# A fused attention and feed-forward kernel: first pair's K side split, loads reordered and released by a new gate, small fillers, joined bursts for all f32-loaded pairs

## The chip, the cores and the metric

One core of one Trainium2 chip runs the whole program. The metric is the device time of one execution in microseconds; "span" is the time from the first to the last instruction of the profiled execution, about 2 us shorter. The kernel before takes 322.0 us (median of 3 runs, 320.87 to 322.46).

## The reference

Random-feature attention (Performer) over 8 batches x 8 heads, then a feed-forward layer with a quick GELU. Two heads make a "pair"; there are 32 pairs, four to a batch.

```python
def phi(x):                       # per pair: K and Q sides
    h = x @ omega.T - sum(x*x)/2;  h = h - max(h)
    return exp(h) / sqrt(m)
kv  = einsum('bhsm,bhsd->bhmd', k_p, v);  z = sum(k_p)
out = einsum('bhsm,bhmd->bhsd', q_p, kv) / (einsum('bhsm,bhm->bhs', q_p, z) + 1e-6)
# then, on x of 4608 x 512:
h = x @ w_in                      # 512 -> 2048
y = (h * sigmoid(1.702 * h)) @ w_out
```

## The kernel before

A scheduler inside the kernel plans, on the host, the order in which each engine gets its instructions; the program is then recorded in that order, and each engine runs its own list strictly in order. A planned order is therefore fixed: an instruction whose data is late holds up everything behind it on its engine. The names of the operations are those of the plan: TK and TQ (transposes of pair i), K and Q (its feature matmuls), KV, ND (numerator and denominator), m1 and m2 (the two feed-forward matmuls, 292 groups of mostly four), hk, hq, hv (f32 loads of a pair), TD (transpose of a pair by DMA), ld (a load on GpSimd's software queue, cast on the way for q, k and weights).

K, Q and KV use half of the array's rows ("tiled"); changing between them and the rest costs time, so they are put in bursts. `mates` says who must stand together:

```python
JOIN, AHEAD = 16, 2
LOADS = [("k", 1), ("q", 1), ("k", 2), ("q", 2), ("k", 3), ("q", 3), ("v", 0), ("v", 1), ("v", 2), ("v", 3)]
LOADS += [("wi", j) for j in range(4)]
LOADS += [(x, i) for i in range(4, 8) for x in "kqv"] + [("wo", j) for j in range(4)]
BEGIN, SPACING = 8, 8        # K of pair i not before so many feed-forward groups
# ...
    def mates(o):
        kind, i = o[0], o[1]
        if kind in ("Q", "KV") and i >= EARLY:
            k = [("K", i + AHEAD)] if JOIN <= i < NPAIR - AHEAD else []
            return k + ([("KV", i)] if kind == "Q" else [("Q", i)] if k else [])
        if kind == "K" and JOIN + AHEAD <= i:
            return [("Q", i - AHEAD), ("KV", i - AHEAD)]
        return []
```

So from pair 16 on, Q and KV of pair i stand in one burst with K of pair i+2. Pairs 1 to 7, v of pair 0 and all weights come through the software queue; k and q of pair 0 and pairs 8 to 31 come as f32 through SP's hardware queue (q of pair 0 through ScalarE's) and are cast by ScalarE or VectorE. The f32 loads begin behind a gate:

```python
deps["gate", 8] = [("ld", "wo", 0)]
# ...
def gate():
    stg[EARLY] = stgp.tile([128, 2 * S], F32, name="stg", tag="stg")
    nc.sync.dma_start(stg[EARLY][:].bitcast(BF16)[:, 2 * S : 2 * S + 2], wout[:, 0, 0:2])
```

The tiny transfer reads the first wout chunk and writes into the tile of pair 8, so the load of k of pair 8, and SP's queue behind it, wait for it.

The softmax here doesn't subtract the row's maximum and nothing guards it: scores larger than these inputs give would overflow.

## Time and profile before

| | before |
|---|---|
| time, median | 322.0 us |
| span of the profiled run | 321.0 us |
| first feed-forward matmul | 20.86 us |
| TensorE busy | 97% |
| last wout chunk landed (from the trace's semaphore records) | 42.4 us |
| TensorE busy, 35 to 57.5 us | 22.01 of 22.50 us |

The lines that carry the reading are in the prediction. Busy time is the sum of an engine's instructions; a matmul's recorded duration overlaps its neighbour's, so for TensorE I read starts, not durations. In lists of waits, the right side of the arrow is what ended the wait. "Issue to landing" of a transfer is from the queue instruction to the last of its semaphore updates.

### The profile page before, as it was taken

To read this page: it belongs to the slowest core of one execution; us is meant where nothing else is said; L and a number is where in the kernel's file an instruction comes from. 1 tells how busy PE (TensorE), PEld (TensorE's weight loads), DVE (VectorE), ACT (ScalarE), POOL (GpSimd) and SP (SyncE) were. 2 spreads that over 40 slices of the span, in tenths; PEclk is the share of its full clock that TensorE was granted. 3 is DMA by queue.
4 is the path that set the end of the run, shared out by engine and by line. 5 is a ranking of instruction groups with operands and counts; after the bars stand their busy time and mean duration, and the time that the engine had idled before them with its cause. 6 is when DMAs were issued, how large, how long until landed. Compare 5 with 4: busy or idle time off the path is not lost.

```text
span 321.0 us, 6636 instructions
## 1 busy us (share of the span) xinstructions
PE 310.8 (97%) x2567; PEld 152.2 (47%) x2567; DVE 179.6 (56%) x341; ACT 202.2 (63%) x379; POOL 59.9 (19%) x98
## 2 busy tenths in 40 slices
PE   6899999999999999999999999999999999999995
PEld 3565554444454444444444454444444444444444
DVE  2878854688558946574666556554635344344300
ACT  3957975788789667866688567666654434434411
POOL 8946311311131211111102030212010000000000
PEclk9999999999999999999999999999999999999999
DMA  8999989999999999999999472323022121111133
GB/s 171 271 222 263 207 253 306 146 300 259 285 191 239 261 242 251 243 237 266 289 263 257 71 134 39 74 54 88 20 56 53 35 59 39 35 33 34 33 88 78
DMA packets 69663, 51.69 MB, mean 161 GB/s; under 512 B 49024, under 2 KB 55168, under 8 KB 69632
## 3 DMA queue, kind: packets, MB, share of 16 engines
q1 hardware_dynamic: 62384, 42.25, 56.4%
q0 software_dynamic: 6880, 8.62, 13.8%
q8 instruction: 20, 0.33, 0.5%
q10 hardware_dynamic: 368, 0.39, 0.4%
q14 instruction: 11, 0.09, 0.1%
HBM read 36.73 MB, written 9.44 MB: 144 GB/s over the span
## 4 chain that ended last, share of the span: by engine, by line
PE 74%; DMA 16%; DVE 3%; issue 2%; ACT 2%; POOL 1%; SPq 1%; ACTq 0%; DVEq 0%; POOLq 0%
PE mo L695 17%; PE mo L721 16%; PE trB L721 12%; PE tr L695 8%; PE trB L695 6%; DMA stg<-in_q_dram 5%; PE tr L721 5%; DMA v<-in_v_dram 4%; DMA wout<-in_moe_w_out_dram 2%; PE nd L657 2%; PE nd L639 2%; DMA stg<-wout 2%; PE pqk L561 2%; DMA xt<-xb 1%; DMA om_f<-in_omega_dram 1%
## 5 line engine op out<-in xcount | busy, mean ns | idle before, releaser
L721 PEld LDWEIGHTS <-gT 128*128 128x128 bf16 x592 | 55.8, 98 | 61.9 <-issue 0.5
L695 PEld LDWEIGHTS <-win 128*128 128x128 bf16 x576 | 53.2, 98 | 61.3 <-issue 2.7
L695 PE MATMUL mo<-xt,win 128*128 128x512 bf16 x316 | 80.2, 379 | 0.4 <-DMA xt<-xb 0.3
L721 PE MATMUL mo<-wout,gT 128*128 128x512 bf16 (+1 forms) x304 | 71.4, 368 | 0.0
L705 ACT ACTIVATE th<-mo 128x512 bf16<-128x512 f32 x79 | 47.5, 606 | 33.9 <-PE mo L695 33.7
L709 DVE SCALAR_TENSOR_TENSOR gT<-th,mo 128x512 bf16<-128x512 bf16 x79 | 53.1, 677 | 27.6 <-ACT th L705 27.3
L721 PE MATMUL trB<-wout,gT 128*128 128x512 bf16 x208 | 51.6, 379 | 0.0
L627 POOL CAST vp<-em 128x9 bf16<-128x9 f32 x31 | 7.3, 235 | 167.8 <-DVE em L619 139.2
L628 POOL TENSOR_TENSOR vp<-v,em 128x576 bf16<-128x576 f32 x31 | 36.0, 1161 | 0.2 <-issue 0.2
L695 PE MATMUL tr<-xt,win 128*128 128x512 bf16 x132 | 33.9, 379 | 0.0
L709 DVE SCALAR_TENSOR_TENSOR gT<-th,tr 128x512 bf16<-128x512 bf16 x33 | 22.5, 681 | 20.3 <-ACT th L705 20.3
L579 ACT ACTIVATE ke<-pqk 128x1024 bf16<-128x1024 f32 x31 | 32.7, 1055 | 0.9 <-PE pqk L561 0.9
L695 PE MATMUL trB<-xt,win 128*128 128x512 bf16 x128 | 32.9, 379 | 0.3 <-DVE gT L709 0.3
L610 DVE TENSOR_TENSOR hm<-ke 128x576 bf16<-128x576 bf16 x32 | 15.8, 492 | 30.5 <-ACT ke L579 29.1
L705 ACT ACTIVATE th<-tr 128x512 bf16<-128x512 f32 x33 | 19.8, 599 | 20.3 <-PE tr L695 20.3
L709 DVE SCALAR_TENSOR_TENSOR gT<-th,trB 128x512 bf16<-128x512 bf16 x32 | 21.8, 680 | 9.9 <-ACT th L705 9.8
L705 ACT ACTIVATE th<-trB 128x512 bf16<-128x512 f32 x32 | 19.4, 608 | 11.4 <-PE trB L695 11.4
L674 DVE TENSOR_TENSOR xb<-nd,r 128x640 bf16<-128x640 f32 x30 | 24.3, 811 | 0.8 <-ACT qe L571 0.5
L614 DVE TENSOR_REDUCE m<-hm 128x9 f32<-128x576 bf16 x32 | 23.9, 747 | 0.3
L541 ACT ACTIVATE qk<-stg 128x1152 bf16<-128x1152 f32 x13 | 15.2, 1168 | 8.3 <-DMA stg<-in_q_dram 8.3
L721 PE MATMUL tr<-wout,gT 128*128 128x512 bf16 x80 | 19.6, 379 | 0.0
L543 DVE CAST qk<-stg 128x1152 bf16<-128x1152 f32 x11 | 8.3, 754 | 18.1 <-DMA stg<-in_q_dram 18.1
(83 smaller groups left out, 283.1 us busy)
## 6 DMA issues: line engine op xcount, KB each, us to landing
out_dram<-osb SPq DMA_DIRECT2D x70, 128.0 KB, 2.4
stg<-in_k_dram SPq DMA_DIRECT2D x25, 288.0 KB, 4.0
stg<-in_q_dram SPq DMA_DIRECT2D x24, 288.0 KB, 4.5
v<-in_v_dram SPq DMA_DIRECT2D x24, 288.0 KB, 4.0
v<-in_v_dram POOLq DMA_DIRECT2D x8, 288.0 KB, 5.6
win<-in_moe_w_in_dram POOLq DMA_DIRECT2D x4, 512.0 KB, 11.3
wout<-in_moe_w_out_dram POOLq DMA_DIRECT2D x4, 512.0 KB, 10.0
qk<-in_k_dram POOLq DMA_DIRECT2D x7, 144.0 KB, 5.6
```

The lines of the kernel that those rows point to most:

```text
L541: nc.scalar.activation(out=dst, in_=src, func=AF.Copy)
L543: nc.vector.tensor_copy(out=dst, in_=src)
L579: nc.scalar.activation(out=st[i]["ke"][:, 1:9, :].rearrange("p (j e) f -> p e j f", e=2), in_=pk[:].rearrange("p e (j f) -> p e j f", f=12 ...
L610: nc.vector.tensor_tensor(out=hm[:], in0=ke[:, :, 0:64], in1=ke[:, :, 64:128], op=ALU.max)
L614: nc.vector.reduce_max(out=m[:], in_=st[i]["hm"][:], axis=AX.X)
L627: e.tensor_copy(out=t[:, :, 64], in_=em[:])
L628: e.tensor_tensor(out=t[:, :, 0:64], in0=v_t[i][:], in1=em[:].unsqueeze(2).to_broadcast([128, NS, 64]), op=ALU.mult,)
L674: nc.vector.tensor_tensor(out=xb[:].rearrange("p g e d -> p e g d"), in0=v4[:, :, :, 0:64], in1=r[:].unsqueeze(3).to_broadcast([128, 2, NG ...
L695: nc.tensor.matmul(dst, lhsT=win[:, c, f * 128 : (f + 1) * 128], rhs=xt[c][:, n * 512 : (n + 1) * 512], start=(c == 0), stop=(c == NC_ - 1),)
L705: nc.scalar.activation(out=t[:], in_=src, func=AF.Tanh, scale=0.851)
L709: nc.vector.scalar_tensor_tensor(out=gts[n][:, f, :], in0=t[:], scalar=1.0, in1=src, op0=ALU.add, op1=ALU.mult)
L721: nc.tensor.matmul(dst, lhsT=gts[n][:, f, m * 128 : (m + 1) * 128], rhs=wout[:, f, w], start=(f == 0), stop=(f == NFC - 1),)
```

## The change

Its intent: let the first pair's K side start before its Q side, put loads in the order in which they are wanted, fill gaps on TensorE with narrower matmuls, and join the bursts of all pairs that are loaded as f32 (8 on, not 16 on). Joining pair 8 wants K of pair 10 early, so the f32 loads are released earlier.

```diff
-LOADS = [("k", 1), ("q", 1), ("k", 2), ("q", 2), ("k", 3), ("q", 3), ("v", 0), ("v", 1), ("v", 2), ("v", 3)]
-LOADS += [("wi", j) for j in range(4)]
-LOADS += [(x, i) for i in range(4, 8) for x in "kqv"] + [("wo", j) for j in range(4)]
+LOADS = "k1 q1 v0 k2 q2 k3 q3 k4 v1 k5 q4 v2 v3 wi0 v4 q5 wo0 k6 wi1 k7 wi2 q6 wi3 v5 q7 v6 wo1 wo2 wo3 v7"
-BEGIN, SPACING = 8, 8
+BEGIN = [4, 8, 11, 20, 48, 56, 59, 70, 73, 81, 85, 88, 88, 96, 96, 131, 131, 144, 151, 155, 157, 172, 188, 193]
-JOIN, AHEAD = 16, 2
+JOIN, AHEAD = 8, 2
@@ the gate of the f32 loads @@
-            nc.sync.dma_start(stg[EARLY][:].bitcast(BF16)[:, 2 * S : 2 * S + 2], wout[:, 0, 0:2])
+            nc.gpsimd.tensor_copy(out=stg[EARLY][0:1, 0:2], in_=wout[0:1, 0, 0:2])
@@ the first pair @@
-            for n, j in enumerate((5, 6, 7, 8, 4)):
+            for n, j in enumerate((5, 6, 7, 8) if i == 0 else (5, 6, 7, 8, 4)):
-            for j in range(4):
+            for n, j in enumerate((4, 0, 1, 2, 3) if i == 0 else range(4)):
+            if i:
+                M(i)      # the ninth slot's two matmuls; for pair 0 they stand before Q
@@ fillers @@
-            for _ in range(n):
-                nc.tensor.matmul(dst, lhsT=zero[:, 0:128], rhs=zero[:])
+            while n > 0:
+                w = 512 if n >= 8 else 128
+                nc.tensor.matmul(dst[:, 0:w], lhsT=zero[:, 0:128], rhs=zero[:, 0:w])
+                n -= w // 128
@@ cut: durations in the scheduler's table, which engine does which copy, order of casts at the start @@
```

More of the change, by code (lines that the diff above doesn't have):

```diff
@@ L50 @@
     "m2": {"P": 0.864},
-    "evK": {"D": 0.400},
+    "evK": {"D": 0.400, "A": 0.640},
     "evQ": {"D": 0.335, "A": 0.478},
@@ L56 @@
     "expQ": {"A": 0.930},
-    "kvs": {"A": 0.160},
+    "kvs": {"A": 0.160, "D": 0.190},
     "tanh": {"A": 0.478},
@@ L67 @@
     "ld": {"G": 0.550},
-    "ck": {"D": 0.370},
-    "TD": {"S": 1.6},
-    "XD": {"S": 1.2},
-    "st": {"S": 0.9},
+    "ck": {"D": 0.370, "A": 0.530},
+    "TD": {"S": 1.5},
+    "XD": {"S": 1.3},
+    "st": {"S": 1.2},
     "hk": {"S": 0.9},
@@ L74 @@
     "hv": {"S": 0.9},
-    "gate": {"S": 0.1},
+    "gate": {"G": 0.1},
     "cast": {"D": 0.740, "A": 1.010},
-    "cq": {"A": 0.530},
+    "cq": {"A": 0.530, "D": 0.370},
+    "ob": {"D": 0.220},
+    "OT": {"P": 0.060},
+    "evO": {"A": 0.250, "D": 0.160},
+    "id": {"G": 0.550},
 }
@@ L81 @@
 FREES = {"evK": "TK", "evQ": "TQ", "evX": "X", "expK": "K", "expQ": "Q"}
-LOADS = [("k", 1), ("q", 1), ("k", 2), ("q", 2), ("k", 3), ("q", 3), ("v", 0), ("v", 1), ("v", 2), ("v", 3)]
-LOADS += [("wi", j) for j in range(4)]
-LOADS += [(x, i) for i in range(4, 8) for x in "kqv"] + [("wo", j) for j in range(4)]
+LOADS = "k1 q1 v0 k2 q2 k3 q3 k4 v1 k5 q4 v2 v3 wi0 v4 q5 wo0 k6 wi1 k7 wi2 q6 wi3 v5 q7 v6 wo1 wo2 wo3 v7"
+LOADS = [(x[:-1], int(x[-1])) for x in LOADS.split()]
 EARLY = 8
+MAIN = {"vp": "G", "evK": "D", "kvs": "A", "ck": "D", "cq": "A", "evO": "A"}
+WARM = 6.5
+FIRST_PAIR = {
+    ("TK", 0): {"P": 0.225},
+    ("TQ", 0): {"P": 0.280},
+    ("K", 0): {"P": 0.225},
+    ("Q", 0): {"P": 0.275},
+    ("evK", 0): {"D": 0.335, "A": 0.530},
+    ("evQ", 0): {"D": 0.400, "A": 0.640},
+}
+START = {"ck": 3.9, "cq": 4.7, "ob": 4.2}
 PORT = (("vp", "G"), ("mx0", "D"), ("cast", "D"))
@@ L88 @@
 FIRST = {"stt": 0, "tanh": 0, "kvs": 0, "rd": 0, "rec": 0, "xm": 1, "evX": 1, "evK": 1, "vp": 1, "expK": 2, "expM": 1, "XD": 0, "TD": 0, "st": 1, "cast": 3}
-BEGIN, SPACING = 8, 8
+BEGIN = [4, 8, 11, 20, 48, 56, 59, 70, 73, 81, 85, 88, 88, 96, 96, 131, 131, 144, 151, 155, 157, 172, 188, 193]
+BACKLOG = 2.5
 XDMA, TDMA = 6, 8
@@ L93 @@
 TILES = [4] * (NBLK - 1) + [5]
-NEAR, LEAD = 14, 22
-TURN = {("expK", 3): -1, ("kvs", 0): 1.5, ("mx0", 2): -2}
-AFTER = [(("evQ", 1), ("expM", 1))]
-ON = {("vp", 0): "G", ("evX", 3): "D"}
+NEAR, LEAD = 14, 20
+TURN = {("ND", 4): 2.5, ("rd", 4): 1, ("X", 0): 1.5, ("expM", 4): 2, ("TQ", 7): 1, ("kvs", 5): 0.5, ("expK", 7): 0.5, ("mx0", 2): -2, ("expQ", 0): 2.5, ("evK", 4): -2}
+AFTER = []
+ON = {("kvs", 4): "D", ("evQ", 0): "D", ("evK", 5): "A", ("evK", 4): "A", ("kvs", 5): "D", ("vp", 1): "G", ("kvs", 0): "D"}
 SLACK = 0.7
-JOIN, AHEAD = 16, 2
+JOIN, AHEAD = 8, 2
 HALT = (1, 2)
@@ L144, in schedule @@
             deps["XD", i] = p("xm")
-    deps["ck", 0], deps["cq", 0] = [], []
-    deps["TK", 0] = [("ck", 0), ("cq", 0)]
+    deps["ck", 0], deps["cq", 0], deps["ob", 0] = [], [], []
+    deps["id", 0] = [("ld", *LOADS[1])]
+    deps["TK", 0] = [("ck", 0), ("id", 0)]
+    deps["TQ", 0].append(("cq", 0))
+    deps["OT", 0] = [("ob", 0), ("TK", 0)]
+    deps["evO", 0] = [("OT", 0)]
+    deps["K", 0].append(("evO", 0))
+    deps["expM", 0] = [("Q", 0)]
     a = {n: [("m1", n, f, c) for f in range(NFC) for c in ["all"]] for n in range(NBLK)}
@@ L177, in schedule @@
         deps["ld", *x] = [("ld", *LOADS[n - 1])] if n else []
+        if n == 2:
+            deps["ld", *x].append(("id", 0))
     deps["gate", 8] = [("ld", "wo", 0)]
@@ L188, in schedule @@
     keep = False
-    begin = [-1] * EARLY + [BEGIN + SPACING * i for i in range(NPAIR - EARLY)]
+    begin = [-1] * EARLY + BEGIN
     order = []
@@ L197, in schedule @@
     ready = {k: {e: 0.0 for e in ENGINES[k[0]]} for k, v in left.items() if not v}
-    free = {"P": 4.0, "A": 2.0, "D": 4.0, "G": 1.2, "S": 8.0}
-    st = {"port": {"D": 0.0, "G": 0.0}, "last": "m2", "tiled": False, "m": 0, "m1": 0, "m2": 0, "dma": 3.2}
+    free = {"P": 1.2, "A": 3.5, "D": 3.5, "G": 1.2, "S": 8.0}
+    st = {"port": {"D": 0.0, "G": 0.0}, "last": "m2", "tiled": False, "m": 0, "m1": 0, "m2": 0, "dma": 4.6}
     banks = {"tr": {"tr0": 0.0, "tr1": 0.0}, "pq": {"pq0": 0.0, "pq1": 0.0}}
@@ L284, in when @@
                 t = max(t, b[0])
-        if kind in ("ck", "cq"):
-            t = 4.0 if kind == "ck" else 4.1
+        if kind in START:
+            t = max(t, START[kind])
+        if kind == "gate":
+            t = fins["ld", "wo", 0]["P"] + 0.3
         if kind == "ld" and len(landed) >= 8:
             t = max(t, landed[-8])
-        if kind == "vp" and o[1] >= 4 and e != "G" or ON.get(o, e) != e:
+        if ON.get(o, e if kind == "vp" and o[1] < 4 else MAIN.get(kind, e)) != e:
             return None
@@ L325, in schedule @@
                     lag = st["m1"] - st["m2"] > LEAD
-                    pref = 0 if att else 1 if (o[0] == "m2") == lag else 2
+                    pref = TURN.get(o, 0) if att else 1 if (o[0] == "m2") == lag else 2
                     key = (start, 0 if tiled and st["tiled"] else 1, pref, t, o[1])
                 elif e == "G":
-                    key = (start, 1 if o[0] == "ld" else 2 if o[0] == "cast" else 0, t)
+                    key = (start, TURN.get(o, 1 if o[0] in ("ld", "id") else 2 if o[0] == "cast" else 0), t)
                 else:
@@ L337, in schedule @@
         start, kind, dur = key[0], o[0], ENGINES[o[0]][e]
+        if o in FIRST_PAIR:
+            dur = FIRST_PAIR[o][e]
+        if e == "P" and kind != "OT" and start < WARM:
+            dur *= 1.9
         if kind in ("m1", "m2"):
@@ L345, in schedule @@
             dur = 0.75 if x[0] in ("wi", "wo") else 0.55
-            size = 2.65 if x[0] in ("wi", "wo") else 0.86
+            size = 2.65 if x[0] in ("wi", "wo") else 0.85
             st["dma"] = max(st["dma"], start + 2.0) + size
@@ L349, in schedule @@
         gap = start - free[e]
-        if e == "P" and gap > 0.5 and st["m"] < 12:
+        early = start < WARM + 2.5
+        if e == "P" and gap > (0.22 if early else 0.5) and st["m"] < 12:
             spare = [(k, x) for k in ("pq", "tr") for x in banks[k] if banks[k][x] is not None and banks[k][x] <= free[e]]
             if spare:
-                order.append((free[e], len(order), ("idle", int((gap - 0.15) / (0.43 if start < 6 else 0.22)), spare[0][1]), "P"))
+                order.append((free[e], len(order), ("idle", int((gap - 0.1) / (0.107 if start < WARM else 0.057)) if early else 4 * int((gap - 0.15) / 0.22), spare[0][1]), "P"))
         free[e] = start + dur
@@ L358, in schedule @@
         if kind in QUEUE:
-            fin = {x: start + dur + (0.0 if x == e else QUEUE[kind]) for x in "PADGS"}
+            late = BACKLOG if kind in ("hk", "hq", "hv") and o[1] >= EARLY + 2 else 0.0
+            fin = {x: start + dur + (0.0 if x == e else QUEUE[kind] + late) for x in "PADGS"}
         elif e != "S":
@@ L362, in schedule @@
         if kind == "ld":
-            fin = {x: landed[-1] for x in "PADS"}
-            fin["G"] = start + dur
+            fin = {x: landed[-1] for x in "PADGS"}
         order.append((start, len(order), o, e))
@@ L412, in schedule @@
             if not w:
-                ready[u] = {x: max(fins[d][x] for d in deps[u]) for x in ENGINES[u[0]]}
+                ready[u] = {x: max((fins[d][x] for d in deps[u] if d[0] != "ld" or u[0] not in ("ld", "id")), default=0.0) for x in ENGINES[u[0]]}
     order.sort()
@@ L475, in load_k, with load_hw @@
             nc.gpsimd.dma_start(qk_t[i][:, S : 2 * S], kv[i])
-        def load_hw(x, i, eng=nc.sync):
+        def load_hw(x, i):
             if x == "v":
@@ L484, in load_hw @@
             else:
-                eng.dma_start(stg[i][:, 0:S], qv[i])
+                nc.sync.dma_start(stg[i][:, 0:S], qv[i])
         def cast(i, eng):
@@ L533, in TQ @@
         def TQ(i, t):
-            for j in range(4):
+            for n, j in enumerate((4, 0, 1, 2, 3) if i == 0 else range(4)):
                 nc.tensor.transpose(
-                    t[:, j * 128 : (j + 1) * 128], qk_t[i][:, j * 128 : (j + 1) * 128], ident[:]
+                    t[:, n * 128 : (n + 1) * 128], qk_t[i][:, j * 128 : (j + 1) * 128], ident[:]
                 )
@@ L545, in evK @@
         def evK(i, t, eng):
-            copy(eng, st[i]["qkT"][:, 0:5, :].rearrange("p n c -> p (n c)"), t[:, 0:640])
+            n = 4 if i == 0 else 5
+            copy(eng, st[i]["qkT"][:, 0:n, :].rearrange("p n c -> p (n c)"), t[:, 0 : n * 128])
         def evQ(i, t, eng):
-            copy(eng, st[i]["qkT"][:, 5:9, :].rearrange("p n c -> p (n c)"), t[:, 0:512])
+            n = 4 if i == 0 else 5
+            copy(eng, st[i]["qkT"][:, n:9, :].rearrange("p n c -> p (n c)"), t[:, 0 : (9 - n) * 128])
         def blk(i, j):
@@ L565, in K, with M @@
                     )
+            if i:
+                M(i)
+        def M(i):
+            t = st[i]["qkT"]
             nc.tensor.matmul(nd[:, 0, 384:512], lhsT=omT[0:64, :], rhs=t[0:64, 4, :])
@@ L586, in Q @@
         def Q(i, pq):
+            if i == 0:
+                M(i)
             t = st[i]["qkT"]
@@ L646, in KV, with kvs @@
                     )
-        def kvs(i, nd):
+        def kvs(i, nd, eng):
             t = work.tile([128, 2, 65], BF16, name="kvs", tag="kvs")
             st[i]["kvs"] = t
-            nc.scalar.activation(out=t[:], in_=nd[:, :, 0:65], func=AF.Copy)
+            copy(eng, t[:], nd[:, :, 0:65])
         def ND(i, nd):
@@ L743, in send @@
                 eng.dma_start(ov[b, SLOT[rank]][:, w], o[64 * h : 64 * h + 64, w])
+        load_hw("k", 0)
         nc.scalar.dma_start(om_f[:], omega[:, :])
-        load_hw("k", 0)
-        load_hw("q", 0, nc.scalar)
+        load_hw("q", 0)
         qk_t[0] = stq.tile([128, 2 * S], BF16, name="qk", tag="qk")
@@ L752 @@
             nc.vector.memset(t[:, :, S:], 1.0)
-        nc.vector.tensor_copy(out=om_b[:, 0, :], in_=om_f[:])
-        nc.vector.tensor_copy(out=om_b[:, 1, :], in_=om_f[:])
         def idle(n, bank):
@@ L777, in emit @@
             elif kind == "ck":
-                nc.vector.tensor_copy(out=qk_t[0][:, S : 2 * S], in_=stg[0][:, S : 2 * S])
+                copy(eng, qk_t[0][:, S : 2 * S], stg[0][:, S : 2 * S])
             elif kind == "cq":
-                nc.scalar.activation(out=qk_t[0][:, 0:S], in_=stg[0][:, 0:S], func=AF.Copy)
+                copy(eng, qk_t[0][:, 0:S], stg[0][:, 0:S])
+            elif kind == "id":
+                make_identity(nc, ident[:])
+            elif kind == "ob":
+                nc.vector.tensor_copy(out=om_b[:], in_=om_f[:].unsqueeze(1).to_broadcast([128, 2, D]))
+            elif kind == "OT":
+                nc.tensor.transpose(nd_b, om_b[:].rearrange("p a d -> p (a d)"), ident[:])
+            elif kind == "evO":
+                copy(eng, omT[:], nd_b)
             elif kind == "ld":
@@ L812, in emit @@
                 t = banks[res["KV", a[0]]]
-                {"KV": KV, "kvs": kvs, "ND": ND, "rd": rd, "xm": xm}[kind](a[0], t)
+                {"KV": KV, "kvs": lambda i, t: kvs(i, t, eng), "ND": ND, "rd": rd, "xm": xm}[kind](a[0], t)
             elif kind in ("hk", "hq", "hv"):
@@ L827 @@
         res = {}
-        for n, (o, eng) in enumerate(schedule(res)):
-            if n == 2:
-                make_identity(nc, ident[:])
-                idle(4, "pq0")
-                nc.tensor.transpose(tr[:, 0:128], om_b[:].rearrange("p a d -> p (a d)"), ident[:])
-                nc.vector.tensor_copy(out=omT[:], in_=tr[:, 0:128])
-                idle(2, "pq0")
+        nd_b = nd[:, 0, 0:64].bitcast(BF16)
+        for o, eng in schedule(res):
             emit(o, eng)
```

## The prediction

> **What bounds the kernel now.** I read the share of busy time first, then the slices, then stretches of the span, then the timeline of the stretch where TensorE is not yet full, then the waits of each engine there.
>
> From the page, busy time and the slices:
>
> ```profile
> PE 310.8 (97%) x2567; PEld 152.2 (47%) x2567; DVE 179.6 (56%) x341; ACT 202.2 (63%) x379; POOL 59.9 (19%) x98
> ...
> PE   6899999999999999999999999999999999999995
> ...
> DMA  8999989999999999999999472323022121111133
> ```
>
> TensorE is busy 97% of 321.0 us; no other engine passes 63%. The DMA engines are full for the first 22 slices (180 us) but slack afterwards, and TensorE is as full in the later slices, so they pace nothing there. Two ends stand out: the first slice, and the last. Cut at the first feed-forward matmul (20.86 us):
>
> ```profile
> core 0: us, PE busy (x) PEld busy (x) DVE busy (x) ACT busy (x) POOL busy (x), PEclk, DMA share, GB/s
> 0.00:20.86 20.86, 16.56 (x225) 10.23 (x226) 13.42 (x37) 13.63 (x25) 16.82 (x32) 1.00 1.06 217
> 20.86:45.00 24.14, 24.05 (x219) 12.12 (x217) 19.72 (x39) 17.64 (x35) 9.59 (x16) 1.00 1.13 231
> 45.00:100.00 55.00, 53.82 (x540) 25.74 (x539) 34.69 (x66) 43.27 (x78) 10.99 (x17) 1.00 1.05 255
> 100.00:180.00 80.00, 79.07 (x676) 38.20 (x675) 50.60 (x96) 58.22 (x114) 13.36 (x20) 1.00 1.06 246
> 180.00:300.00 120.00, 120.00 (x820) 56.74 (x819) 59.29 (x104) 65.11 (x124) 9.11 (x14) 1.00 0.26 55
> 300.00:321.00 21.00, 17.34 (x97) 9.19 (x94) 1.90 (x3) 4.35 (x8) 0.00 (x0) 0.97 0.27 63
> ```
>
> So there are two regimes. Before 20.86 us TensorE waits or runs fillers on zeros, and a chain through ScalarE and VectorE sets the time. After it TensorE is the bound: only what shortens its own stream, or its waits, moves the end. The feed-forward matmuls there (1152 of 512 columns, counting half-width ones in pairs) stand 216 ns apart: 248.8 us that the change does not touch. The last matmul ends 3.7 us before the end, also untouched.
>
> What else is in the stream shows in the timeline of TensorE:
>
> ```profile
> 55.54 0.40 PE L561 MATMUL pqk<-omT,qkT 64*128 64x128 bf16 x8
> 55.78 0.22 PE L566 MATMUL nd<-qkT,omT 64*128 64x128 bf16 x1
> 55.78 0.22 PE L567 MATMUL nd<-omT,qkT 64*128 64x128 bf16 x1
> 55.93 1.04 PE L721 MATMUL mo<-wout,gT 128*128 128x512 bf16 x4
> 56.80 1.03 PE L721 MATMUL tr<-wout,gT 128*128 128x512 bf16 x4
> 57.76 0.40 PE L561 MATMUL pqk<-omT,qkT 64*128 64x128 bf16 x8
> ```
>
> Read the starts, since the durations overlap. Four full matmuls followed by four more take 56.80 - 55.93 = 0.87 us; followed by a half-array burst (64 rows) they take 57.76 - 56.80 = 0.96. Entering costs about 96 ns (single starts: 312 against 216 ns). Leaving costs nearly as much: from a KV matmul to a full one 121 ns, to a half-array one 26. I use 95 ns per change of mode.
>
> **What the Trainium skill says.** "TensorEngine Tiling (Array Packing)", Key Properties, says that changing the tiling mode, not just the tile, drains TensorE. The trace agrees, with 95 ns above. "TensorE: Matmul & The Clock Gate", What's actually happening, says that the clock is halved until TensorE has been busy about 3.4 us. The trace agrees: fillers of 512 columns start about 0.43 us apart at 1.2 to 5 us and 0.22 apart at 24 us; pair 0's eight K matmuls last 0.61 us where later ones last 0.40. "DMA: Bandwidth & Descriptors", Queues, rings and completion order, says that a DMA engine takes turns between the rings that have work, a packet at a time. The trace agrees where a tiny transfer met the software queue's traffic:
>
> ```profile
> 34.80 0.56 SPq L493 DMA_DIRECT2D stg<-wout  x1
> 41.23 0.34 SPq L483 DMA_DIRECT2D stg<-in_k_dram  x1
> ```
>
> This gate took 6.4 us to land. Its packets (22 ns each) began at 38.7 and took 0.9 us for some nine per DMA engine: about 100 ns each, one of the other queue's packets (98 ns) between every two.
>
> **The change part by part.** What follows is from the built order of instructions, which says nothing of time, and from the durations above.
>
> 1. Joined bursts from pair 8 on instead of 16: K of pair i+2, Q and KV of pair i stand together. Bursts fall from 55 to 42. Counted after the first feed-forward matmul, changes of mode fall from 92 to 64: 28 x 0.095 = **2.7 us less**, on the path, as TensorE is full there.
>
> 2. Work moved ahead of the first feed-forward matmul: transposes of pairs 4 and 5, K and Q of pair 4. Spacings: five transposes of 56 ns, 0.28 us, and four, 0.22; K 0.28; Q 0.23. Sum 2 x 0.50 + 0.51 = **1.5 us less** afterwards, provided the first matmul does not come later for it.
>
> 3. Fillers among the feed-forward matmuls are gone: two of 216 ns and a wait of 0.1: **0.5 us less**. At the start the fillers become 128 columns wide, so real work need not stand behind a 0.43 us one.
>
> 4. The prelude. Before, the first pair's K transposes waited until 5.66 us behind fillers, though the cast ended at 5.21; VectorE first cast omega twice. After, K is cast first (about 3.9 to 4.4), four transposes follow at about 4.5, the copy ends near 5.5, K starts near 5.8 (7.18 before) and its exponential near 6.4 (8.27 before). But then ScalarE and VectorE bind, and they get more to do before the first feed-forward matmul:
>
> ```profile
> L604 ACT ACTIVATE qe<-pq 128x1024 bf16<-128x1024 f32 x3 | 3.3, 1103 | 0.0
> L579 ACT ACTIVATE ke<-pqk 128x1024 bf16<-128x1024 f32 x3 | 3.2, 1059 | 0.0
> ...
> L570 ACT ACTIVATE ke<-nd 128x128 bf16<-128x128 f32 x4 | 1.2, 308 | 0.7 <-PE nd L567 0.7
> ```
>
> Back to back these start 0.90, 0.90 and 0.16 us apart. Pair 4 adds 0.90 + 0.90 + 2 x 0.16 = 2.1 us to ScalarE; the second v product on VectorE (0.6), one kvs (0.2) and more copies (0.40 each) go to VectorE. Walking both queues in the new order with such spacings I get VectorE done with the third pair's product at about 19.4, ScalarE with its last copy at about 20.9, and, after ND of pair 3 and nine transposes, the first feed-forward matmul at 21.2 us. Before, the first stood at 20.86, but with gaps: three had run when the stream became gapless at 22.26, and a transpose of 0.28 between them, so the effective start was 22.26 - 0.65 - 0.28 = 21.3. I count **0.1 us less**, give or take 0.8: the earlier start is spent on the moved work.
>
> 5. The loads. Thirteen loads instead of ten precede the first chunk of the first weight (win), and one of the second weight (wout) comes before win's second. Before, software loads landed at about 0.83 us for q or k, 0.78 for v and 2.5 for a weight chunk, from 4.0 us on. Added up in the new order, the four win chunks land at 17.4, 24.8, 28.1 and 31.4 us. The new PE order wants them at about 21, 26.5, 30 and 34.6. That fits alone. But the gate is now a GpSimd copy after the first wout chunk, about 23 us, so the f32 loads of pairs 8 to 11 start some 15 us sooner, against the software queue. Sharing packet by packet, with the gate's 3.9 us to first packets, leaves wi2 in time but puts wi3 at about 36 and the last wout chunks 1 to 2 us late. I charge **1.5 us more** (0 to 5).
>
> 6. Later waits. The steps between matmuls that exceed their usual spacing after 45 us sum to about 3.0 us (0.56 at 51, 0.76 at 70, 0.42 at 127, 0.78 at 151, 0.45 at 156). The new irregular spacing of the pairs is evidently fitted to remove some; joined bursts need two free PSUM banks at once, which caused the one at 151 (Q behind a ScalarE store). I take **0.6 us less**.
>
> Sum: -2.7 - 1.5 - 0.5 - 0.1 + 1.5 - 0.6 = -3.9. From the timed median, 322.0, this gives 318.1; I round to 318.0.
>
> **The rivals.** (a) The DMA engines become the bound between 25 and 50 us. For it: their share is already over 1 there, and total work is conserved, so f32 loads started early delay weights. Against it: k, q, v loads are few before pair 12 for want of buffers, and all queues drain sooner. Fully true, it costs 5 us: about 321.5. (b) The prelude really gets shorter, because VectorE's copies overlap more than I walked, and the later waits vanish: 1.5 + 2 us further gain, 314.5. For it: pair 0 has a 1.5 us lead; against it: ScalarE was already gapless for most of 8 to 18 us, and carries more. (c) Joining eight more pairs trades switches for waits on banks or on K of two pairs ahead: half of the 2.7 is lost, 319.5. For it: the wait at 151; against it: sixteen joined bursts show little other waiting.
>
> **Range and chances.** The certain parts (switches, moved work, fillers) are 4.7 us, 1.5%. Faster by over 2% needs below 315.6, so 2.4 us from waits and prelude together: 0.2. Slower by over 2% needs 11 us of new waits: 0.01. Range 314.2 to 321.3.
>
> **What would show it.** Step 1: mean spacing of feed-forward matmuls down, 13 fewer bursts. Step 2 and 4: a gapless stream from 20.5 to 22 us with pair 4's Q done; if it starts at 19.5, I walked the queues too slowly. Step 5: TensorE waits for DMA of win or wout between 25 and 50 us; none means the charge was wrong. Step 6: waits beyond 45 us near 2.4 us. The prediction is wrong if such waits pass 5 us, or if the prelude moves by over 2 us either way.

## The result, and the profile after

The changed kernel takes **326.5 us** (median of 4 runs, 325.84 to 328.07) against 322.06 for the kernel before (4 runs). The ratio is 1.0151 with a 95% interval of 1.0104 to 1.0199: it is slower by 1.5%. A ratio is the mean time of one kernel's fast runs over that of the other's fast runs of the same rounds, so it is not quite the ratio of the medians. The predicted range ended at 321.3.

From the page of the changed kernel, busy time, slices and the last part, on the issues of transfers:

```profile
PE 308.2 (95%) x2582; PEld 153.3 (47%) x2582; DVE 176.2 (54%) x337; ACT 206.2 (64%) x392; POOL 58.8 (18%) x97
...
PE   7879875999999999999999999999999999999995
...
PEclk9999998999999999999999999999999999999999
DMA  8999999999999999998995452222162211111223
...
wout<-in_moe_w_out_dram POOLq DMA_DIRECT2D x4, 512.0 KB, 20.8
```

The same last line of the page of the kernel before:

```profile
wout<-in_moe_w_out_dram POOLq DMA_DIRECT2D x4, 512.0 KB, 10.0
```

TensorE has a hole in slices 5 to 7 (32 to 57 us), with a fall of its clock in the last, and the chunks of the second weight take twice as long to land. The stretches of the changed kernel, columns as in the prediction:

```profile
35.00:57.50 22.50, 15.39 (x149) 7.50 (x147) 11.81 (x23) 11.94 (x22) 3.82 (x5) 0.93 1.16 245
57.50:100.00 42.50, 42.50 (x401) 21.16 (x400) 27.28 (x54) 29.92 (x62) 9.52 (x14) 1.00 1.06 264
100.00:180.00 80.00, 80.00 (x727) 39.27 (x726) 50.04 (x95) 65.35 (x125) 12.42 (x20) 1.00 0.98 230
```

Beside it the kernel before:

```profile
35.00:57.50 22.50, 22.01 (x242) 11.29 (x240) 13.30 (x29) 16.76 (x30) 3.90 (x6) 1.00 1.05 255
```

In 22.5 us TensorE does 15.4 us of work instead of 22.0, while the DMA engines are fuller (1.16 against 1.05). Afterwards it has no gap at all. To put both on one scale I count, for every matmul that has started, its usual spacing (216 ns for a full one, 56 a transpose, 31.6 an ND, 16.5 a KV, 28 a K, 113 a Q), and call the rest of the time lost: waits, fillers and changes of mode.

| stretch | lost, before | lost, after | difference |
|---|---|---|---|
| 0 to 35 us | 15.2 | 14.7 | -0.5 |
| 35 to 57.5 us | 2.3 | 10.3 | +8.0 |
| 57.5 us to the last matmul | 9.2 | 4.7 | -4.5 |
| sum | 26.7 | 29.7 | +3.0 |

The last matmul starts at 317.1 us before and 320.1 after, which agrees. So the steady part gained what was hoped for and more, and one stretch of 22 us gave it back nearly twice. Whom TensorE waits for in the changed kernel:

```profile
PE pqk L593 <- DMA qkT<-qk: 3.0, 1, 3.0
PE mo L760 <- DMA wout<-in_moe_w_out_dram: 2.8, 3, 1.3
PE tr L559 <- DMA qk<-in_q_dram: 1.8, 2, 1.2
```

All three are transfers. None of them was among TensorE's waits before, where the one DMA wait was 0.3 us. The timeline of TensorE shows them one after another:

```profile
45.95 1.02 PE L760 MATMUL mo<-wout,gT 128*128 128x512 bf16 x4 [1.14 <-DMA wout<-in_moe_w_out_dram]
...
49.25 1.02 PE L760 MATMUL mo<-wout,gT 128*128 128x512 bf16 x4 [1.29 <-DMA wout<-in_moe_w_out_dram]
...
53.56 0.40 PE L593 MATMUL pqk<-omT,qkT 64*128 64x128 bf16 x8 [2.98 <-DMA qkT<-qk]
...
54.36 1.86 PE L760 MATMUL mo<-wout,gT 128*128 128x512 bf16 x4 [0.34 <-DMA wout<-in_moe_w_out_dram]
56.02 1.86 PE L760 MATMUL trB<-wout,gT 128*128 128x512 bf16 x4
```

The last two lines show a second price: four full matmuls last 1.86 instead of about 1.03 us. Soon after the wait of 2.98 us the clock fell: the granted clock was 0.50 from 54.29 to 57.70 us, and eight matmuls stand 427 instead of 216 ns apart, 1.7 us in all.

The queue of SP in the changed kernel tells what the early release did:

```profile
34.04 7.51 SPq L548 DMA_TRANSPOSE qkT<-qk  x1
41.60 0.56 SPq L515 DMA_DIRECT2D stg<-in_q_dram  x1
42.27 7.52 SPq L548 DMA_TRANSPOSE qkT<-qk  x1
```

Merely issuing the transpose of pair 8 kept SP 7.5 us, and it landed 19.5 us after its start. The packet records show where the 19.5 us went. For 8.7 us (to 42.8) it stood in SP's queue behind the f32 loads. Then its 1,152 packets of 256 bytes took 9.9 us, where in the kernel before, with the software queue empty, the same number took 2.4 us. The queues from 44 to 50 us (packets, MB, share of the 16 engines' time):

```profile
q0 software_dynamic: 881, 0.90, 88.0%
q1 hardware_dynamic: 872, 0.22, 30.1%
```

One packet of the weights went for each small packet of the transpose. Landing times from the semaphore records, in us:

| | before | after |
|---|---|---|
| first f32 load behind the gate issued | 41.2 | 25.2 |
| win, fourth chunk | 23.5 | 36.8 |
| wout chunks 1 to 4 | 34.8, 37.3, 39.9, 42.4 | 22.7, 45.9, 49.2, 54.3 |
| transpose of pair 8 by DMA | 53.6 | 53.5 |
| q of pair 8, q of pair 10 | 44.8, 50.7 | 30.8, 41.5 |
| last load of pair 11's q and k | 54.3 | 55.1 |

This is the heart of it. The f32 loads were released 16 us sooner, and most landed 8 to 14 us sooner. But pair 8's transpose, without which its loads are of no use, landed when it had landed before, and so did pair 11's last load, which stood behind that transpose in SP's queue. The transfer engines were full all along, so the time that the early loads got was taken from the weights and the transposes. (Part of the weights' lateness is the new order of loads: e5 below, with the same order and a later gate, has the fourth win chunk at 32.8 and the wout chunks at 23.3, 37.5, 40.0 and 43.7.) The plan had counted on the early loads: the kernel's own scheduler, run on the host, puts K of pair 8 at 44.4 us (53.0 in the kernel before), and it ran at 53.6.

One oddity of the changed kernel shows at 1.66 us of the same queue:

```profile
1.66 0.43 SPq L513 DMA_DIRECT2D stg<-in_k_dram  x1
```

This is the k load of pair 8. The new gate writes columns 0 and 1 of the tile, which belong to q; the k half is not held by it and loads ahead of pair 1. In this trace pair 1's q landed at 8.0 us instead of 6.5 (but at 6.6 in e7 and e12, which have the same stray load).

### The profile page after: what moved, and what is told of

It is laid out like the page before. It is cut to its first block, busy times and chain, and to the rows that moved or that the text cites.

```text
span 324.1 us, 6673 instructions
## 1 busy us (share of the span) xinstructions
PE 308.2 (95%) x2582; PEld 153.3 (47%) x2582; DVE 176.2 (54%) x337; ACT 206.2 (64%) x392; POOL 58.8 (18%) x97
## 4 chain that ended last, share of the span: by engine, by line
PE 82%; DMA 13%; POOL 3%; issue 1%; ACT 0%; POOLq 0%; ACTq 0%
PE mo L760 23%; PE mo L734 16%; PE trB L734 12%; PE tr L760 11%; DMA wout<-in_moe_w_out_dram 8%; PE tr L734 7%; PE trB L760 5%; DMA win<-in_moe_w_in_dram 4%; PE nd L696 2%; PE nd L678 2%; DMA qk<-in_q_dram 2%; PE pqk L593 2%; PE mo L629 1%; PE tr L629 1%; PE trB L629 1%
## 5 line engine op out<-in xcount | busy, mean ns | idle before, releaser
L760 PE MATMUL mo<-wout,gT 128*128 128x512 bf16 (+1 forms) x368 | 87.0, 373 | 2.8 <-DMA wout<-in_moe_w_out_dram 2.8
L734 PEld LDWEIGHTS <-win 128*128 128x128 bf16 x576 | 53.9, 98 | 62.5 <-DMA win<-in_moe_w_in_dram 0.6
L734 PE MATMUL mo<-xt,win 128*128 128x512 bf16 x276 | 69.7, 379 | 0.2
L744 ACT ACTIVATE th<-mo 128x512 bf16<-128x512 f32 x69 | 41.7, 610 | 31.4 <-PE mo L734 30.3
L748 DVE SCALAR_TENSOR_TENSOR gT<-th,trB 128x512 bf16<-128x512 bf16 x49 | 33.5, 685 | 35.2 <-ACT th L744 35.1
L734 PE MATMUL trB<-xt,win 128*128 128x512 bf16 x196 | 50.4, 379 | 0.0
L744 ACT ACTIVATE th<-trB 128x512 bf16<-128x512 f32 x49 | 29.8, 609 | 20.9 <-PE trB L734 20.8
L760 PE MATMUL tr<-wout,gT 128*128 128x512 bf16 x160 | 40.3, 379 | 0.0
L571 ACT ACTIVATE qk<-stg 128x1152 bf16<-128x1152 f32 (+1 forms) x19 | 21.8, 1150 | 8.5 <-DMA stg<-in_q_dram 8.5
L734 PE MATMUL tr<-xt,win 128*128 128x512 bf16 x104 | 26.7, 379 | 0.0
L774 ACT ACTIVATE osb<-mo 128x512 f32<-128x512 f32 (+1 forms) x23 | 13.5, 589 | 10.1 <-PE mo L760 10.0
L696 PEld LDWEIGHTS <-qe 128*128 128x128 bf16 x320 | 14.0, 97 | 6.7 <-issue 0.2
```

What stands on the lines that cost most here:

```text
L571: nc.scalar.activation(out=dst, in_=src, func=AF.Copy)
L696: nc.tensor.matmul(nd[:, e, g * 65 : (g + 1) * 65], lhsT=qe[i % NQE][:, e, g * 128 : (g + 1) * 128], rhs=t[:, e, :],)
L734: nc.tensor.matmul(dst, lhsT=win[:, c, f * 128 : (f + 1) * 128], rhs=xt[c][:, n * 512 : (n + 1) * 512], start=(c == 0), stop=(c == NC_ - 1),)
L744: nc.scalar.activation(out=t[:], in_=src, func=AF.Tanh, scale=0.851)
L748: nc.vector.scalar_tensor_tensor(out=gts[n][:, f, :], in0=t[:], scalar=1.0, in1=src, op0=ALU.add, op1=ALU.mult)
L760: nc.tensor.matmul(dst, lhsT=gts[n][:, f, m * 128 : (m + 1) * 128], rhs=wout[:, f, w], start=(f == 0), stop=(f == NFC - 1),)
```

## The experiments

Theory 1: the early release of the f32 loads makes them take turns with the weights' packets, so weights and transposes land late and TensorE, which runs in order, stands; joining from pair 8 on is what asked for the early release. Theory 2: the new plan itself (its order, its banks) costs the time. Twelve kernels ran. In the traces of e5 to e12 about 40 of some 2,580 matmul records are missing, so TensorE's busy time is slightly too low there.

### e1: the kernel before, with the early release alone

```diff
-            elif kind == "gate":
-                gate()
+            elif kind == "gate":
+                pass                      # and gate() right after the load of q of pair 6
-            nc.sync.dma_start(stg[EARLY][:].bitcast(BF16)[:, 2 * S : 2 * S + 2], wout[:, 0, 0:2])
+            nc.gpsimd.tensor_copy(out=stg[EARLY][0:1, S : S + 2], in_=win[0:1, 0, 1536:1538])
```

> The kernel before, TensorE's order of instructions unchanged, but the f32 loads of pairs 8 to 11 are let go at about 24 us (a GpSimd copy after the fourth win chunk) instead of 41 us. Theory 1 (the early f32 loads take turns with the weights' packets and make weights and transposes late): the wout chunks land at 45 to 55 us instead of 35 to 42, TensorE waits for wout between 42 and 57 us, and the time rises by 3 to 8 us to 325 to 330. Theory 2 (the new plan itself, not the early release, costs the time): within 1 us of 322. Theory 3 (early loads help): below 321.

Measured: 325.16 us against 321.57, ratio 1.0111 (1.0056 to 1.0166). TensorE's order is the same instruction for instruction. The wout chunks landed at 41.7, 45.6, 48.2 and 51.1 us. TensorE's longest waits and the stretch:

```profile
PE mo L721 <- DMA wout<-in_moe_w_out_dram: 4.2, 3, 1.8
```

```profile
35.00:57.50 22.50, 18.28 (x206) 9.44 (x205) 12.82 (x26) 14.60 (x26) 3.94 (x7) 1.00 1.06 216
```

It follows that the early release by itself, with no other part of the change, costs 3.6 us (1.8 to 5.3 by the interval), and that it costs them where Theory 1 says. A rival is that the gate, now a GpSimd instruction that waits, held up the software queue behind it. The trace speaks against it: the wout chunks were issued 0.3, 0.3, 0.7 and 1.5 us later than before, but landed 6.9 to 8.7 us later. Pair 8's k and q landed at 30.0 and 31.8 us instead of 44.1 and 44.8, and yet its transpose landed at 52.1 instead of 53.6: its cast keeps its place in ScalarE's unchanged order and ran at 44.2 (44.9 before).

### e2: the kernel after, with ten of the early f32 loads taken away

The result is wrong: pairs 9 to 11 are cast from pair 8's q and k, and pairs 8 to 11 use v of pairs 4 to 7.

```diff
+            if EARLY <= i < EARLY + 4 and (x == "v" or i > EARLY):
+                if x == "v":
+                    v_t[i] = v_t[i - 4]
+                else:
+                    stg[i] = stg8[0]
+                return
```

> The kernel after with TensorE's order unchanged, but ten of the eleven f32 loads that meet the weights' traffic are taken away (q and k of pairs 9 to 11 are cast from pair 8's, v of 8 to 11 from 4 to 7; result wrong on purpose). Theory 1: the waits between 35 and 57 us shrink from some 8 us to under 2, the clock does not fall, and the time goes from 326.5 to 317 to 321. Theory 2 (the plan's order or its PSUM banks cost the time): it stays at 325 to 327.

Measured: 318.04 us, ratio 0.9887 (0.985 to 0.9923), with the same order on TensorE as the kernel after. The stretch:

```profile
35.00:57.50 22.50, 21.63 (x247) 11.53 (x246) 15.96 (x32) 17.84 (x35) 6.50 (x9) 1.00 1.26 237
```

21.63 us of work instead of 15.39, and the clock stays at 1.00. Theory 2 falls as the explanation of the loss: with the traffic thinned, the new plan is 8.5 us faster than it was, and faster than the kernel before.

### e3: the gate on the k half

```diff
-            nc.gpsimd.tensor_copy(out=stg[EARLY][0:1, 0:2], in_=wout[0:1, 0, 0:2])
+            nc.gpsimd.tensor_copy(out=stg[EARLY][0:1, S : S + 2], in_=wout[0:1, 0, 0:2])
```

> The kernel after, except that the gate writes the first column of the k half of the tile, not of the q half, so that the k load of pair 8 can no longer run at 1.7 us, ahead of pair 1's. Theory 1: pair 1's loads land 0.6 to 0.8 us sooner, the first feed-forward matmul comes 0.3 to 0.8 us sooner, but the stall between 35 and 57 us stays: 325.3 to 326.3. Rival (the stray load is what upsets everything): below 322.

Measured: 326.5 us, ratio 1.0146 (1.0108 to 1.0184), no change from after. Pair 1's q landed at 6.3 instead of 8.0 us and the first feed-forward matmul came at 22.1 instead of 22.7. That this half microsecond is the stray load's is not shown: e7 and e12, which have the stray load and the same order up to there, began at 21.5. The end did not move: between 35 and 57.5 us TensorE lost 10.8 us by the count above (10.3 in after; its busy time of 16.4 us is at a mean clock of 0.85, not 0.93), in waits for wout, a transpose and q as in after, and here for a win chunk too (1.5 us). In these runs, with that bound further on, the earlier start was worth nothing.

### e4: late gate, joined from pair 10 on

```diff
-    deps["gate", 8] = [("ld", "wo", 0)]
+    deps["gate", 8] = [("ld", "wo", 2)]
-JOIN, AHEAD = 8, 2
+JOIN, AHEAD = 10, 2
+            st["hw"] = max(st["hw"], start + 1.7) + {"TD": 1.1, "XD": 0.7}.get(kind, 0.75)   # scheduler's queue
@@ cut: the gate's tile column and chunk, load sizes in the scheduler @@
```

> The kernel after with the gate on the third wout chunk (about 40 us) and on the k half, pairs joined from 10 on, replanned by the kernel's own scheduler with queue spacings taken from the trace. Theory 1: no stall beyond 2 us between 35 and 60 us, and the time is 316 to 320, below both kernels. Theory 2: 324 or more.

Measured: 331.53 us, ratio 1.0306 (1.0252 to 1.036). The expectation failed. The stall between 35 and 57.5 us is gone (22.50 of 22.50 us busy), but it came back later:

```profile
PE mo L734 <- DVE gT L748: 5.5, 5, 1.9
PE nd L678 <- DVE xb L713: 2.2, 1, 2.2
PE mo L734 <- DMA xt<-xb: 1.5, 1, 1.5
```

Between 57.5 and 130 us TensorE was busy for 62.5 of 72.5 us. From pair 12 on the pairs ran later than the scheduler had planned, up to 13 us late by pair 16, and the waits named are those of a plan whose pairs come too late, not of one slow engine. Two things had been changed here that could do this: pairs joined before their loads are there, and the scheduler's shorter queue times. The next runs take them apart.

### e5: late gate, and joining and spacing as before

```diff
-    deps["gate", 8] = [("ld", "wo", 0)]
+    deps["gate", 8] = [("ld", "wo", 1)]
-BEGIN = [4, 8, 11, 20, 48, 56, 59, 70, 73, 81, 85, 88, 88, 96, 96, 131, 131, 144, 151, 155, 157, 172, 188, 193]
+BEGIN = [8 + 8 * i for i in range(24)]
-JOIN, AHEAD = 8, 2
+JOIN, AHEAD = 16, 2
@@ cut: the gate's tile column and chunk @@
```

> The kernel after with its gate held until the second wout chunk has landed (about 39 us instead of 23), on the k half, and with what asked for early pairs taken back: joined bursts from pair 16 on and pairs spaced by eight as before; replanned. 92 changes of mode become about as many as before. Theory 1 (the early release is the loss, and joining from pair 8 on is what asked for it): no stall above 1 us between 35 and 57 us, no crowd of waits between 57 and 130 us as in the run e4, time 317 to 321. Theory 2 (something else in the new plan costs): 324 or more.

Measured: 319.14 us, ratio 0.9917 (0.9889 to 0.9945): correct, and faster than both kernels. The stretch:

```profile
35.00:57.50 22.50, 22.18 (x203) 11.30 (x206) 10.21 (x21) 12.63 (x22) 2.86 (x5) 1.00 1.01 246
```

Issuing pair 8's transpose takes SP 1.3 us here. And the plan holds: every K and every ND of all pairs starts within 0.7 us of where the scheduler put it, whereas in the kernel after all of them from pair 9 on start 11 to 12 us late. What the scheduler leaves out, but for a fixed 2.5 us from pair 10 on, is that the two queues share engines. Its later gate still lets the f32 loads go at 37.7 us, before the 41.2 of the kernel before.

### e6: the kernel before, joined from pair 8 on

```diff
-JOIN, AHEAD = 16, 2
+JOIN, AHEAD = 8, 2
```

> The kernel before with one number changed: joined bursts from pair 8 on, gate and loads as before. Theory 1 (a joined burst needs K of the pair two further on, so pair i is finished only when pair i+2 has been loaded; with the loads let go at 41 us TensorE waits): fewer changes of mode, but waits of 4 to 9 us between 57 and 130 us; time 324 to 331. Rival (joining is worth its 2.7 us by itself): 318 to 320.

Measured: 327.21 us, ratio 1.0166 (1.0138 to 1.0194). Between 57.5 and 130 us TensorE was busy for 66.6 of 72.5 us, against 71.6 before. It waits mainly for a product of VectorE (2.4 us) and for gT (1.5). It follows that joining is no gain by itself while the loads come at 41 us: pair i is finished only when K of pair i+2 can run, so a joined plan needs its pairs earlier. This is why the change came with an early gate.

### e7: the kernel after, joined only from pair 16 on

```diff
-JOIN, AHEAD = 8, 2
+JOIN, AHEAD = 16, 2
```

> The kernel after, gate early as it is, but joined only from pair 16 on. Theory 1: the stall between 35 and 57 us is there as in after, since loads and gate are the same, so the time is 325 to 329 and the steady part loses 1 to 2 us in changes of mode. Rival (joining causes the stall by itself): 321 or less.

Measured: 328.31 us, ratio 1.0223 (1.0166 to 1.0281), with 15.18 us of work between 35 and 57.5 us. The stall is there without the joining, so the bursts are not needed for it; e9 tests the release.

### e8: late gate, unjoined, but with the scheduler's shorter queue times

It is e5 with the gate on the fourth wout chunk and e4's queue times in the scheduler.

> As e5, but with the gate on the last wout chunk and the scheduler's queue spacings from the trace (a load each 0.75 us). Theory 1: wout as early as in before, waits between 35 and 57 us under 1 us, time 317 to 321; if the scheduler now counts on pairs too early, some waits beyond 60 us, and up to 325.

Measured: 333.32 us, ratio 1.0359 (1.0317 to 1.0402), outside what I expected. Between 35 and 57.5 us TensorE is as full as in e5 (22.18 us), but between 57.5 and 130 it is busy for 64.1 of 72.5. Since e8 is not joined, joining alone is not what spoiled e4. The shorter queue times and the later gate are the two differences from e5; with them the plan counts on pairs too early, and in-order engines then stand. Which of the two weighs more stays open. The longer constants of the changed kernel (4.5 us from issue to landing, 2.5 more from pair 10 on) are what held in e5.

### e9: e5 with the early gate

```diff
-    deps["gate", 8] = [("ld", "wo", 1)]
+    deps["gate", 8] = [("ld", "wo", 0)]
@@ and the same index in the planned time and in what the copy reads @@
```

> The kernel e5 with three places changed back: the gate of the f32 loads waits for the first wout chunk (about 23 us) instead of the second (about 39 us). Pair spacing and joining are those of e5, so this is the early release alone. Theory 1 (early release makes weights and transposes late): against e5's 319.1 us the time rises by 5 to 11 us to 324 to 330, with TensorE waits for win, wout or transposes between 35 and 60 us. Rival (the pair spacing and joining were what cured e5): within 2 us of e5.

Measured: 328.73 us, ratio 1.024 (1.0195 to 1.0285). This is the cleanest pair: one index apart, 9.6 us between the medians, or 10.4 by the two ratios (1.024 / 0.9917 = 1.0326, times 319.1). The waits:

```profile
PE pqk L593 <- DMA qkT<-qk: 3.7, 1, 3.7
PE mo L760 <- DMA wout<-in_moe_w_out_dram: 2.8, 2, 1.4
PE tr L559 <- DMA qk<-in_q_dram: 1.4, 1, 1.4
```

They are the waits of the kernel after, in the same order, and its first transpose took 20.2 us to land. The scheduler replans around the earlier release, so the two orders differ, but only in answer to it. That answer is part of the 9.6 us: it puts K of pair 8 at 44.4 us, where e5's plan has it at 56.5, and TensorE reached it and then waited for the transpose until 54.1.

### e10 and e11: two plans searched with the late gate

Loads, spacing and joining (from pair 11 and from pair 13) were searched with the kernel's own scheduler, with its own queue times and the gate on the second wout chunk.

> A candidate that should beat both: late gate (second wout chunk), loads, pair spacing and joining (from pair 11) searched again with the kernel's own scheduler, which was right within 0.7 us for every pair of e5. Theory 1 (with no contention the plan holds on the chip): 316 to 318.5, no wait above 1.5 us. If the search leans on timings that the plan has wrong: 320 or more.

> Another candidate of the same search, joined from pair 13 and with first weight later (all k, q of pairs 4 to 6 before it). Theory 1: 316 to 318.5; if its loads of weights come late on the chip, waits for win and 320 or more.

Measured: 318.89 us (ratio 0.9933, 0.9886 to 0.9981) and 318.98 us (0.9935, 0.9884 to 0.9987). Both beat the kernels before and after, neither can be told from e5, and both lie 0.4 to 0.5 us above the range that I expected. Joining from 11 or 13 can be afforded with the late gate, but the search's further gains in the plan did not show on the chip.

### e12: e2 with joining only from pair 16 on

This asks what joining is worth where no load is late. The result is wrong, as in e2.

```diff
-JOIN, AHEAD = 8, 2
+JOIN, AHEAD = 16, 2
```

> The kernel e2 (after without ten of the early f32 loads, result wrong on purpose) with joined bursts from pair 16 on, so that both have no contention: what joining pairs 8 to 15 is worth by itself. After the first feed-forward matmul it has 80 changes of mode against 64 in e2, 16 x 0.095 = 1.5 us. Theory (the 95 ns are the whole worth): the time is 1 to 2.5 us over e2's 318.0, that is 319 to 320.5. Rival (the transfers' lateness hid the worth, or waits eat it): within 0.5 us of e2 or below it.

Measured: 319.78 us, ratio 0.9949 (0.9935 to 0.9963), against 0.9887 for e2: 0.0062 of 321.5, or 2.0 us (1.7 by the medians). For 16 changes of mode that is 105 to 125 ns each, near the 95 read from the trace. Two cautions: the intervals of the two ratios leave anything from about 0.7 to 3.3 us, and the waits are not the same (1.6 us for a transpose and 1.4 for xt in e12, 0.9 and 0.9 in e2, which has one of 1.0 for q instead). So joining is worth about what the prediction said where its loads are in time; the cost of a change is not measured closer than that.

## Why the prediction was wrong

**Step 1, joined bursts, held.** It gave 2.7 us for 28 changes of mode. Of the 4.5 us gained after 57.5 us, 18 fewer changes there (49 against 67) are 1.7 us; e12 finds 1.7 to 2.0 us for 16 changes, with the cautions given there.

**Step 6, later waits, held and was too small.** It took off 0.6 us. The waits after 57.5 us, 2.4 us before, vanished in the kernel after. That they vanished because of the new spacing is argued, not shown: in e5, with the old spacing, two such waits are there again (0.8 and 0.6 us, both for ScalarE, at 94 and 95 us). A kernel that is late everywhere by 11 us also has its data early.

**Steps 2 to 4, the start, were too hopeful.** They summed to 2.1 us; the table shows 0.5 by 35 us. The step that failed in this trace is "the first feed-forward matmul at 21.2 us": it came at 22.7. I did not see the stray load of pair 8's k in the diff, but e7 and e12, with the same load and the same order up to there, began at 21.5, inside my "give or take 0.8". So the trace differs by 1.2 us from executions that should start alike, and whether the walk of the queues was wrong stays open.

**Step 5, the loads, is where the prediction failed.** It said "I charge 1.5 us more (0 to 5)"; the stretch lost 8.0 us more than before. The mechanism was right, and the one landing worked out for the shared queues was close: the fourth win chunk "at about 36" came at 36.8 (the first three came 1.2 to 1.6 us after their times). What failed was the step from landings to waits, in three terms. First, "puts ... the last wout chunks 1 to 2 us late" was counted as one lateness, but TensorE waited 1.1 us for the second chunk, 1.3 for the third and 0.3 for the fourth. With the waits in between, the fourth was wanted some 7 us before it could be used (an estimate: 1.2 + 1.1 + 1.3 + 3.0 + 0.3). Second, the transposes by DMA were left out. They share the same hardware queue, take 7.5 us to issue and 19.5 to land instead of 2.0 and 6.7, and pair 8's K alone waited 3.0 us for one. q of pair 7 cost another 1.2. Third, the fall of the clock after the long wait, 1.7 us, was left out. Rival (a) described this outcome and still put it at 321.5, with the same three terms missing.

**What I should have seen** is in the prediction's own views. The DMA share was over 1 in every stretch up to 180 us. With the engines full, the early release could bring pairs 8 to 11 forward only by pushing back what shared the engines, and TensorE's order wanted those weights first. e1 measures that push with the order fixed: 3.6 us. e9 against e5 gives 9.6 us, because the order too was planned on the early loads: of its waits, 3.7 us are for pair 8's transpose, which e1 does not have, and its clock was at 0.50 for 6.8 us (not at all in e1). How the 9.6 us divide was not tested.

What stays open: what TensorE would gain if only the transpose's turns with the weights (9.9 us), or only its stand behind the f32 loads (8.7 us), were taken away; no run separates them. The gains of e5 over the kernel before (2.8 us) were not split into start, gate and fillers either.

## What to carry to other kernels

When the transfer engines are full, releasing a group of loads earlier brings it forward only at the cost of whatever shares the engines (here pair 8's q came 14 us sooner, and it did not help, since the transpose behind it did not), so ask what is displaced before asking what is advanced. A planned order for in-order engines is only as good as its model of the queues: let the plan be compared with the trace, operation by operation, and where the two part is the place to look. And a saving on the bound engine that needs its data earlier (here a burst that waits for the pair two further on) must be priced with those loads in it.

## What the Trainium skill lacked or had wrong

- "DMA: Bandwidth & Descriptors", Queues, rings and completion order, has the turns between rings, and the trace agrees (881 and 872 packets of the two queues from 44 to 50 us). It does not say what follows for the queue that issues: a transpose by DMA that stood behind f32 loads, with the software queue busy, kept SP's queue for 7.5 us (1.3 in e5), and the loads behind it waited as well.
- "DMA: Bandwidth & Descriptors" gives no time for a transpose under such sharing: 19.5 us from issue to landing in the kernel after, against 6.7 in the kernel before and 3.2 in e5.
- "TensorEngine Tiling (Array Packing)", Key Properties, says that a change of mode drains TensorE, without a cost. The trace gives about 95 ns for each change; e12 against e2 gives 105 to 125, with noise and some waits in it.
- "TensorE: Matmul & The Clock Gate", What's actually happening, gives one idle window of about 3.4 us for the fall of the clock. Here a stretch that was not wholly idle was enough: in the 3.41 us before the fall at 54.29 us TensorE was busy for 0.45 us, and in e9, in the 3.41 us before the fall at 50.97 us, for 1.51 us. The page has nothing on how much work in a window still lets the clock fall.
- No page that I found says how many transfers the software queue holds, and these runs do not show it either. In both traces GpSimd waited at a load until the one eight earlier had landed (in the kernel before, k of pair 6 was issued at 21.50 us, after the third win chunk's landing at 20.96), but that may be the program's own semaphores, not the queue.
